# An attention and long-convolution kernel: the transform of 768 split into 3 by 256, with even and odd frequencies in separate rows

## The chip, the core and the metric

The kernel runs on one core of one Trainium2 chip. The metric is device microseconds for one launch. Five engines share the work: PE (matrix products), DVE (VectorE), ACT (ScalarE), POOL (GpSimd), and SP, which here only issues DMAs. Each engine works through its own instructions in order and waits on semaphores for the others.

## The reference, cut to what matters

```python
# q, k, v: [4, 8, 768, 64]; heads 0, 2, 6 see all earlier rows, the others 4 sink rows and a window of 64
a = softmax(mask(q @ k.T / 8)); x = (a @ v) as [4, 768, 512]
proj = x @ w_proj                      # [4, 768, 1536]
x1, x2, x3 = proj[..., :512], proj[..., 512:1024], proj[..., 1024:]
X2 = rfft(x2, n=768, axis=1)
H  = rfft(filter_fft, n=768, axis=0)
y  = x1 * irfft(X2 * H, n=768, axis=1) * x3
return y @ w_out                       # [4, 768, 512]
```

## The kernel before, in words

The work is 16 head pairs, numbered n, four to a batch b. A pair has two heads of one of three kinds: both see everything (RR), both are local (LL), or one of each (RL); the order in a batch is RR, LL, RL, LL. Everything is built in the function `patterned` as named operations; `run` issues them in the order of two lists of words, AHEAD and FAST. A word such as `E0.1/v` is operation E of pair 0, part 1, on VectorE (`/s` ScalarE, `/p` GpSimd), and `sc0.1@4` puts its result into PSUM banks from number 4. Each engine's queue is the list's order, kept to that engine's words; these lists were planned ahead, so the order of the whole kernel is fixed by hand, and a changed operation means a new list.

For a pair: `lq`, `lk`, `lv` load, `cq`, `ck`, `cv` cast to bf16, `T` and `E` turn q and k (from pair 8 on, T is a DMA transpose on SP's queue), `kx`, `ks`, `vx`, `vs` gather the keys and values that local heads need, `sc` makes scores, `ex` their exponentials on ScalarE (line 1471), `at` the products with the values (1516), `rec` and `nm` normalize (1522, 1533). Masks come in two ways: for pairs below BIASED_FAST, `sb` adds -32768 to scores by a product on PE (1465), and for the others `mk` and `mr` multiply the exponentials by 0 or 1 on VectorE or GpSimd (1484 to 1503).

Then comes the transform along the 768 rows, in a real form: `fd` and `fe` take the difference and the sum of the two halves of the rows, `fA`, `fS`, `fb`, `fr` combine thirds of these (1549 to 1561), and `W` multiplies by tables of cosines and sines on PE (1569 to 1573), `We` evicts. For each batch, `X` multiplies the spectrum by the middle third of w_proj (1620), in three parts t of two tiles of 512 channels, and `Xe` evicts to bf16. `pa`, `pb`, `pc` multiply by the spectrum of the filter (tile HAB) as complex numbers; in part 2, rows 0 to 63 hold one member of the pair and rows 64 to 127 the other, so that two DMAs `sw` swap halves of rows (1645) for `pb`. The inverse transform `c` is six products of 384 columns for each of four blocks of channels cb (1685), three for the even and three for the odd half; `ce` evicts one half to f32, `cv{b}.{cb}.0` and `.1` add and subtract (1696).

The projections x1 and x3 use `tn`, the attention result turned (by PE and `te`, or by a DMA transpose), four products of 384 columns for each half (1655); `xs` evicts x1 and `g` multiplies by x3 straight out of PSUM (1674). `y` multiplies by the convolution. `o` multiplies by w_out (1712), `oe` evicts and `st` stores (1732, 1734).

At the start the kernel makes its tables from sines (`fcol`, `turns`, `angle`, `wrap`, `size`, `sin`, `cos`, `G..`, `Gm..`, `Gh..`, `Gk..`, and `Gt`, `Ge`, which transpose the forward table for the inverse, 1227 and 1231), and transforms the filter: `lfilt`, `fold`, eighteen products `F` of 512 columns (1265), scalings `H` into HAB (1272, 1274), and two DMAs `Hd`. `blank` are products of nothing, laid among the first loads. The helpers `ev`, `two` and `scale` record their instructions at lines 971 to 978 and 1159 to 1163.

## Time and profile before

| | us |
|---|---|
| three timed runs | 195.18, 189.86, 193.86 (median 193.86) |
| the profiled execution | 190.27 |
| its span, first to last instruction | 188.4 |
| PE, DVE, ACT, POOL busy within the span | 176.5, 161.2, 145.6, 69.0 |
| mean granted TensorE clock | 0.985 |

The profile is one execution. Busy time is the union of an engine's instructions; ends of matrix products are modelled, so the pace of PE is better read from the chain of work that ended last, where products follow each other without a wait. In the groups of instructions a row gives line, engine, operation, output and input tiles, shapes and count, and behind the bar busy us, mean ns of one, and the idle time just ahead of them.

### The profile page before, as it was taken

The numbers are of one execution on the slowest core, as the hardware profiler recorded it, in microseconds if no ns is written. First come the engines' busy times: TensorE is split into PE (matmuls) and PEld (weight loads), VectorE is DVE, ScalarE is ACT, GpSimd is POOL, SyncE is SP. The second block draws the span as 40 slices with busy tenths as digits, with TensorE's granted clock in tenths as the row PEclk, the third lists the DMA queues.
The fourth block names the chain that finished last, engine by engine and source line by source line (L and its number), as shares of the span: only waits on it lengthen the run. The fifth ranks groups of instructions, "written<-read, shape, count | busy, mean of one in ns | idle before, by whom it ended". The sixth has DMA issues, their size and how long they took to land.

```text
span 188.4 us, 4493 instructions
## 1 busy us (share of the span) xinstructions
PE 176.5 (94%) x1694; PEld 103.4 (55%) x1694; DVE 161.2 (86%) x329; ACT 145.6 (77%) x210; POOL 69.0 (37%) x103
## 2 busy tenths in 40 slices
PE   7879999989998999999999999999999999999970
PEld 2437664647745563575555656655657765555530
DVE  6887799789889999999989999999899996499810
ACT  5787899999999999988989999696977332426360
POOL 5874785554322224670250460700650630000000
PEclk9978999999999999999999999999999999999997
DMA  4999999999999999999999989982162002312074
GB/s 152 330 274 279 208 197 236 270 286 251 213 202 225 215 185 166 233 219 213 202 233 228 228 221 238 250 87 56 60 98 111 3 2 111 135 36 111 11 286 157
DMA packets 78955, 34.01 MB, mean 180 GB/s; under 512 B 68306, under 2 KB 75218, under 8 KB 78930
## 3 DMA queue, kind: packets, MB, share of 16 engines
q1 hardware_dynamic: 75986, 30.81, 73.9%
q0 software_dynamic: 2944, 2.88, 9.1%
q8 instruction: 14, 0.23, 0.5%
q14 instruction: 11, 0.09, 0.2%
HBM read 24.64 MB, written 6.29 MB: 164 GB/s over the span
## 4 chain that ended last, share of the span: by engine, by line
PE 66%; ACT 14%; DVE 6%; DMA 5%; issue 3%; POOL 2%; SPq 2%; DVEq 0%; ACTq 0%; POOLq 0%
PE space L1655 18%; PE space L1712 11%; PE space L1620 8%; PE space L1452 7%; PE space L1685 7%; PE space L1516 6%; ACT f_pT L1471 4%; DMA f_qkT<-f_qk_bf 3%; ACT f_HAB L1274 3%; DMA f_v_f<-in_v_dram 2%; PE space L1465 2%; ACT f_qk_bf L975 2%; SPq L1383 2%; PE space L1569 1%; PE space L1571 1%
## 5 line engine op out<-in xcount | busy, mean ns | idle before, releaser
L1471 ACT ACTIVATE f_pT<-space 128x1024 bf16<-128x1024 f32 (+3 forms) x68 | 58.8, 917 | 6.1 <-PE space L1465 1.9
L1655 PE MATMUL space<-f_xT,f_wproj 128*128 128x384 bf16 x256 | 47.9, 326 | 0.1
L1655 PEld LDWEIGHTS <-f_wproj 128*128 128x128 bf16 x256 | 24.0, 98 | 17.1 <-issue 1.0
L1712 PE MATMUL space<-f_wout,r_gy 128*128 128x512 bf16 x96 | 24.7, 379 | 0.0
L1452 PE MATMUL space<-f_qkT 64*128 64x128 bf16 (+3 forms) x248 | 22.6, 253 | 1.1 <-DVE f_attn L1533 0.5
L1620 PE MATMUL space<-f_wproj,f_xh 128*128 128x512 bf16 x96 | 22.7, 379 | 0.1
L1685 PE MATMUL space<-f_Gi,r_P 128*128 128x384 bf16 x96 | 19.0, 326 | 0.7 <-ACT f_evs L975 0.3
L978 DVE TENSOR_TENSOR f_pT<-f_pT,r_mtab 128x1024 bf16<-128x1024 bf16 (+3 forms) x33 | 18.5, 583 | 0.8 <-ACT f_pT L1471 0.6
L975 ACT COPY f_o<-space 128x1024 f32<-128x1024 f32 (+1 forms) x12 | 9.9, 836 | 11.3 <-PE space L1712 11.2
L1516 PEld LDWEIGHTS <-f_pT 128*128 128x128 bf16 x472 | 16.7, 97 | 3.6 <-issue 0.9
L1516 PE MATMUL space<-f_v_aug,f_pT 128*128 128x65 bf16 x392 | 17.9, 193 | 0.6 <-ACT f_X L975 0.5
L1452 PEld LDWEIGHTS <-f_qkT 64*128 64x128 bf16 x248 | 10.3, 94 | 13.1 <-issue 10.4
L978 POOL TENSOR_TENSOR f_uv<-f_fo 128x256 bf16<-128x256 bf16 x12 | 9.1, 766 | 21.1 <-DVE f_fo L978 15.8
L1696 DVE TENSOR_TENSOR f_conv<-f_evs,space 128x384 bf16<-128x384 f32 x32 | 16.1, 545 | 0.6 <-PE space L1685 0.3
L975 ACT CAST f_xh<-space 128x768 bf16<-128x768 f32 x14 | 11.2, 808 | 4.9 <-PE space L1573 4.6
L1620 PEld LDWEIGHTS <-f_xh 128*128 128x128 bf16 x96 | 9.0, 98 | 10.0 <-issue 0.4
L1712 PEld LDWEIGHTS <-r_gy 128*128 128x128 bf16 x96 | 9.0, 98 | 8.9 <-issue 0.4
L1533 DVE TENSOR_TENSOR f_attn<-space,f_rec 128x768 bf16<-128x768 f32 x14 | 13.4, 955 | 0.4
L1685 PEld LDWEIGHTS <-r_P 128*128 128x128 bf16 x96 | 8.8, 97 | 7.4 <-issue 1.1
L978 POOL TENSOR_TENSOR f_fo<-f_attn 128x384 bf16<-128x384 bf16 x11 | 10.4, 960 | 2.4 <-DVE f_attn L1533 1.9
L975 ACT CAST f_X<-space 128x1024 bf16<-128x1024 f32 x8 | 8.2, 1020 | 2.8 <-PE space L1620 2.7
L978 POOL TENSOR_TENSOR f_pT<-f_pT,r_mtab 128x512 bf16<-128x512 bf16 (+1 forms) x6 | 6.8, 1146 | 9.1 <-ACT f_pT L1471 9.1
(136 smaller groups left out, 345.7 us busy)
## 6 DMA issues: line engine op xcount, KB each, us to landing
f_v_f<-in_v_dram SPq DMA_DIRECT2D x32, 192.0 KB, 4.7
out_dram<-f_o SPq DMA_DIRECT2D x9, 512.0 KB, 3.1
r_qk_f<-in_k_dram SPq DMA_DIRECT2D x10, 192.0 KB, 4.4
r_qk_f<-in_q_dram SPq DMA_DIRECT2D x10, 192.0 KB, 5.0
r_qk_f<-in_k_dram SPq DMA_DIRECT2D x4, 384.0 KB, 11.3
r_qk_f<-in_q_dram SPq DMA_DIRECT2D x4, 384.0 KB, 6.1
f_qk_f<-in_q_dram SPq DMA_DIRECT2D x4, 384.0 KB, 5.8
f_qk_f<-in_k_dram SPq DMA_DIRECT2D x4, 384.0 KB, 6.6
```

Source lines behind the costliest of these rows:

```text
L975: nc.scalar.copy(out=out, in_=in_)
L978: (nc.gpsimd if now["engine"] == "p" else nc.vector).tensor_tensor(out, a, b, op)
L1274: nc.scalar.activation(out=out_(), in_=in_(), func=AF.Copy, scale=w / S)
L1452: nc.tensor.matmul(sc[:, bank, col:col + 128 * cnt], lhsT=keys, rhs=qkT(n)[rows, 0, 128 * i:128 * (i + cnt)], start=(col == 0 or not biase ...
L1471: nc.scalar.activation(out=pT(n)[:, c, :, 0:w], in_=held[f"sc.{n}.{c}"][:, :, 0:w], func=AF.Exp, scale=SCALE)
L1516: nc.tensor.matmul(att[:, hh, 65 * i:65 * i + 65], lhsT=pT(n)[:, c, bank, col:col + 128], rhs=values, start=(z == 0), stop=(z == len(here) ...
L1533: nc.vector.tensor_mul(attn(n).rearrange("p i hh d -> p hh i d"), rows[:, :, :, 0:64], held[f"rec.{n}"][:, :, :, None].to_broadcast([128, ...
L1620: nc.tensor.matmul(ps[:, u, :], lhsT=xh(b)[:, cc, chain, 128 * part:128 * part + 128], rhs=wproj()[:, cc, DM:2 * DM], start=(cc == 0), sto ...
L1655: nc.tensor.matmul(ps[:, s, 0:HS], lhsT=wproj()[:, cc, part * DM + cb * 128:part * DM + (cb + 1) * 128], rhs=xT(b)[:, cc, s * HS:s * HS + HS],
L1685: nc.tensor.matmul(ps[:, 0, 0:HS], lhsT=P(b)[:, t, u, ch], rhs=Gi()[:, tile_no], start=(m == 0), stop=(m == 2))
L1696: fn(conv[:, half * HS:half * HS + HS], held[f"evs.{b}.{cb}"], held[f"c_ps.{b}.{cb}.1"][:, 0, 0:HS])
L1712: nc.tensor.matmul(ps, lhsT=gy(b)[:, cb, i * 128:(i + 1) * 128], rhs=wout()[:, cb, :], start=(cb == 0), stop=(cb == NC - 1))
```

## The change

The 768 rows are treated as 3 by 256. Frequencies of one parity are gathered in one set of rows, so that each of the three spectrum parts is a whole complex number per row: part 0 holds one class modulo 3, parts 1 and 2 the other two.

- Tables: a forward table of 6 tiles instead of 18, and two small inverse tables Gi and Gj of 256 columns, made straight from the sines. The steps skew, Gm, Gh and the transposes Gt with Ge are gone; the angle table is 512 columns wide instead of 384.
- Filter: it goes through the same sixths as the pairs (`fAF`, `fSF`, `fbF`, `frF`), 24 products `K` with evictions `Ke`, 24 transposes `F`, and scalings `H` of 512 columns. The DMAs `Hd` are gone. `gate` makes GpSimd wait for pair 3's q before the filter and weight loads.
- Pairs: `We` sorts the spectrum into six groups of 128. The forward products stay as they are.
- After the filter multiplication nine operations q form the three points of the transform of length 3: sums and differences of parts 1 and 2 (`qa`, `qs`), a correction of one row (`qr`), half of part 0 (`qh`), the sums (`qz`, `qb`, `qp`, `qm`) and a scaling (`qd`). The DMAs `sw` are gone.
- Inverse: for each cb six products of 256 columns instead of six of 384. In batches 0 to 2 `y` multiplies straight out of PSUM; in batch 3 ScalarE evicts first (`cv3.cb/s`). `ce` and the two halves `cv` are gone.
- The rows of the convolution now come sorted by class modulo 3: `xs` and `g` read x1 and x3 from PSUM with a step of three, and each store writes every third row of the output.
- BIASED_FAST 4 becomes 8: pairs 4 to 7 get their masks from PE (15 more `sb`) and lose `mk`, `mr`. Pair 14's `tn` becomes a DMA transpose.
- Both order lists are new, with other engines for some casts and evictions: among them three more `xs`, one more `nm`, one more `te` on ScalarE; on GpSimd four `mk` fewer, and `qa0`, `qd1`, `qd2`, `fbF` more. The blanks are still twelve in FAST, and now all stand among the first operations.

The core of the diff (the order lists cut to the end stage):

```diff
-TURNED_BACK = (0, 1, 2, 3, 4, 5, 6, 7, 14, 15)
+TURNED_BACK = (0, 1, 2, 3, 4, 5, 6, 7, 15)
-BIASED_FAST = 4
+BIASED_FAST = 8
+DIRECT = ((0, 0), (0, 1), (0, 2), (0, 3), (1, 0), (1, 1), (1, 2), (1, 3), (2, 0), (2, 1), (2, 2), (2, 3))
...
-X3.2.0 X3.1.0@0 Xe3.2/s X3.1.1 sw3.0 pa3.2/v sw3.1 x33.1.1 Xe3.1/s X3.0.0@2 g3.1 X3.0.1 pb3.1/v pa3.1/v
-x33.2.1@4 Xe3.0/s pb3.2/v o2.1.0@0 pa3.0/v o2.1.1 x13.3.1@6 pc3.1/v o2.0.0 pc3.2/v o2.0.1 x33.2.0 pb3.0/v
-oe2.1/s c3.0.0@2 pc3.0/v x13.3.0 st2.1 ce3.0/s g3.2 c3.0.1@3 xs3.3/s c3.1.1@0 cv3.0.0 c3.1.0@1 cv3.0.1 c3.2.0@2
...
+o2.4.0 o2.4.1 oe2.1/s X3.2.0@6 st2.1 X3.2.1 X3.1.0@0 Xe3.2/s X3.1.1 pb3.2/v X3.0.0@2 pa3.2/v Xe3.1/s x13.0.0@6
+pc3.2/v oe2.5/s pb3.1/v X3.0.1 pa3.1/v st2.5 x13.0.1 Xe3.0/s pc3.1/v x13.3.0@0 xs3.0/s pa3.0/v x13.2.0@4 qa3/v
+x13.3.1 pb3.0/v x33.0.0@2 xs3.3/s qs3/v x13.1.0@6 pc3.0/v qr3/s x33.0.1 qh3/v x13.1.1 g3.0 x33.1.1@0 qd3/s qb3/v
+x33.1.0 qz3/v x13.2.1 xs3.1/s qp3/v x33.2.1@2 xs3.2/s qm3/v x33.2.0 g3.1 c3.0@6 g3.2 c3.1@4 cv3.0/s c3.2@0
+cv3.1/s y3.0/v c3.3@2 cv3.2/s y3.1/v x33.3.1@6 cv3.3/s y3.2/v x33.3.0 y3.3/v o3.5.0@4 g3.3 o3.2.0@5 o3.5.1
...
+    def spectrum(ps, u, uv, br, ch):
+        nc.tensor.matmul(ps[:, u, 0:256], lhsT=br[:, 1, u, ch], rhs=G()[:, 3 * u:3 * u + 2], start=True, stop=False)
+        nc.tensor.matmul(ps[:, u, 0:256], lhsT=uv[:, 2 * u, ch], rhs=Gk()[:, u], start=False, stop=True)
+        nc.tensor.matmul(ps[:, u, 256:384], lhsT=br[:, 0, u, ch], rhs=G()[:, 3 * u + 2], start=True, stop=True)
+
+    def sorted_(x, ps):
+        ev(x.rearrange("p g (u j) -> p u g j", u=2), ps[:, :, 0:HS].rearrange("p u (g j) -> p u g j", g=6))
...
+            ps = banks(f"F_ps{t}", BF16, 1)
+            for c, g in enumerate(SPECTRUM[t]):
+                for cc in range(NC):
+                    nc.tensor.transpose(ps[:, 0, DM * c + 128 * cc:][:, 0:128], Hx()[:, cc, g], identity())
...
-                two(P(b)[:, t], held[f"X.{b}.{t}"], HAB()[:, t, 0:2], ALU.mult)
+                h = HAB()[:, t, 0:1].to_broadcast([128, 2, DM]) if t else HAB()[:, t, 0:2]
+                two(P(b)[:, t], held[f"X.{b}.{t}"], h, ALU.mult)
...
-                nc.sync.dma_start(out=Xw[to], in_=held[f"X.{b}.2"][at])
+        @op(f"qa{b}")
+            two(SD(b)[:, 0:2], P(b)[:, 1], P(b)[:, 2], ALU.add)
+        @op(f"qs{b}")
+            two(SD(b)[:, 2:4], P(b)[:, 1], P(b)[:, 2], ALU.subtract)
+        @op(f"qr{b}")
+            scale(SD(b)[0:1], flat(b)[0:1, 2:6], 2.0)
+        @op(f"qh{b}")
+            scale(Y0(b), P(b)[:, 0], 0.5)
+        @op(f"qz{b}")
+            two(Y0(b), Y0(b), SD(b)[:, 0:4:3], ALU.add)
+        @op(f"qd{b}")
+            scale(SD(b)[:, 1:3], SD(b)[:, 1:3], 2.0 * KAPPA)
+        @op(f"qb{b}")
+            two(P(b)[:, 0], P(b)[:, 0], SD(b)[:, 0:4:3], ALU.subtract)
+        @op(f"qp{b}")
+            two(flat(b)[:, 2:4], P(b)[:, 0], SD(b)[:, 1:3], ALU.add)
+        @op(f"qm{b}")
+            two(flat(b)[:, 4:6], P(b)[:, 0], SD(b)[:, 1:3], ALU.subtract)
...
-                    ps = banks(f"c_ps.{b}.{cb}.{r}", count=1)
-                    for m, (t, u, tile_no) in enumerate(INVERSE[r]):
-                        nc.tensor.matmul(ps[:, 0, 0:HS], lhsT=P(b)[:, t, u, ch], rhs=Gi()[:, tile_no],
-                                         start=(m == 0), stop=(m == 2))
+                for s, (re, im) in enumerate(POINTS):
+                    for c, rows in enumerate((re, im)):
+                        rhs = Gi()[:, c].rearrange("p a f -> p (a f)")[:, START[s]:START[s] + 256] if s else Gj()[:, c]
+                        nc.tensor.matmul(ps[:, 256 * s:256 * s + 256], lhsT=rows(b)[:, ch], rhs=rhs,
+                                         start=(c == 0), stop=(c == 1))
...
+                    nc.vector.tensor_mul(to, held[f"c_ps.{b}.{cb}"].rearrange("p a f -> p (a f)")[:, 0:S], x)
...
+                    rows = out[b].rearrange("(n p s) c -> s p n c", p=128, s=3)[i // 2]
```

469 lines of the change are left out of this document (227 added, 242 removed).

## The prediction

> **What bounds the kernel now.** I read the page's busy shares first, then the same by stage, cut where the bounding engine changes, then the chain for the true pace of PE.
>
> ```profile
> PE 176.5 (94%) x1694; PEld 103.4 (55%) x1694; DVE 161.2 (86%) x329; ACT 145.6 (77%) x210; POOL 69.0 (37%) x103
> ```
>
> ```profile
> 0.00:20.00 20.00, 17.10 (x130) 8.79 (x131) 15.43 (x40) 14.76 (x22) 13.82 (x37) 0.91 0.95 260
> 20.00:79.00 59.00, 55.65 (x664) 34.40 (x663) 53.61 (x108) 57.73 (x77) 26.27 (x34) 1.00 1.12 221
> 79.00:159.20 80.20, 80.20 (x780) 48.26 (x779) 74.92 (x156) 62.55 (x98) 28.89 (x33) 1.00 0.78 153
> 159.20:182.80 23.60, 23.53 (x124) 11.90 (x122) 17.20 (x27) 10.05 (x15) 0.00 (x0) 1.00 0.30 104
> 182.80:188.40 5.60, 0.00 (x0) 0.00 (x0) 0.00 (x0) 0.55 (x1) 0.00 (x0) 0.79 0.49 182
> ```
>
> The columns after the length are busy PE, weight loads, DVE, ACT, POOL. The reader is to see three regimes. From 20 to 79 us ScalarE works 57.73 of 59.00 us: its exponentials, casts and evictions set the pace. From 79 to 159.2 PE is full and DVE has 74.92 of 80.20. After 159.2 PE alone is full. At 182.8 PE is done; the last output tile and its store take 5.6.
>
> A full PE row can still hide slack, because matmul ends are modelled. The chain shows the pace when nothing waits:
>
> ```profile
> 20.18 1.30 PE space L1516 x42
> 28.13 0.34 PE space L1589 x6
> 30.45 1.51 ACT f_HAB L1274 x2
> ...
> 75.41 0.94 DVE f_conv L1696 x2
> ...
> 83.19 4.58 PE space L1655 x28
> ...
> 144.00 0.49 PE space L1685 x3
> 159.16 0.86 PE space L1620 x4
> 177.55 5.19 PE space L1712 x24
> ```
>
> The columns are start and length. A product of 65 columns takes 31 ns, 128 columns 56, 384 columns 163, 512 columns 216; 256 columns, which stand on that line, I take at 108. The ACT and DVE rows show that consecutive instructions overlap: two conv halves take 0.94 us, not twice 0.545. I subtract 0.085 us from each duration below when I add a queue. Counted with these paces along the order list, PE's whole work is 158.0 us, of which 58.2 stand ahead of the last exponential of head pair 8 and 99.8 behind it.
>
> ```profile
> 78.33 0.60 ACT L1471 ACTIVATE f_pT<-space 128x512 bf16<-128x512 f32 x1
> ```
>
> This row of the timeline is that exponential, done at 78.9 us. PE finishes 103.9 us later: only 4.1 us of slack for 99.8 of work. The 21 us that PE loses lie before it, under ScalarE's regime.
>
> **The change part by part.** The prices come from these groups (busy us, mean ns):
>
> ```profile
> L1696 DVE TENSOR_TENSOR f_conv<-f_evs,space 128x384 bf16<-128x384 f32 x32 | 16.1, 545 | 0.6 <-PE space L1685 0.3
> L975 ACT CAST f_xh<-space 128x768 bf16<-128x768 f32 x14 | 11.2, 808 | 4.9 <-PE space L1573 4.6
> L978 DVE TENSOR_TENSOR r_P<-r_P,f_m 128x1024 bf16<-128x1024 bf16 x12 | 8.2, 687 | 0.1
> L971 DVE COPY f_qkT<-space 128x768 bf16<-128x768 bf16 x8 | 7.6, 950 | 0.9 <-PE space L1407 0.9
> L1674 DVE TENSOR_TENSOR r_gy<-r_x1s,space 128x768 bf16<-128x768 bf16 x8 | 7.5, 942 | 0.3 <-PE space L1655 0.3
> L978 DVE TENSOR_TENSOR f_uv<-f_fo 128x256 bf16<-128x256 bf16 x20 | 7.5, 392 | 0.1
> L975 ACT COPY f_evs<-space 128x384 f32<-128x384 f32 x14 | 6.8, 493 | 3.1 <-DVE f_conv L1696 2.2 <-PE space L1685 0.8
> L975 ACT CAST f_qk_bf<-r_qk_f 128x768 bf16<-128x768 f32 x8 | 6.5, 831 | 1.0 <-DMA r_qk_f<-in_q_dram 1.0
> L975 ACT COPY f_qkT<-space 128x768 bf16<-128x768 bf16 x8 | 6.2, 802 | 0.1
> L978 DVE TENSOR_TENSOR r_gy<-f_conv,r_gy 128x768 bf16<-128x768 bf16 x10 | 5.7, 569 | 0.1
> L1530 ACT ACTIVATE f_attn<-space,f_rec 128x64 bf16<-128x64 f32 x24 | 5.1, 344 | 0.0
> L971 DVE COPY f_xT<-space 128x768 bf16<-128x768 bf16 x8 | 4.3, 550 | 0.6 <-PE space L1589 0.6
> L1274 ACT ACTIVATE f_HAB<-space 128x1024 bf16<-128x1024 f32 x2 | 2.1, 1041 | 0.1
> L1274 ACT ACTIVATE f_HAB<-space 128x512 bf16<-128x512 f32 x2 | 1.2, 598 | 0.0
> L975 ACT COPY f_Gi<-space 128x768 bf16<-128x768 bf16 x1 | 0.8, 793 | 0.0
> ```
>
> PE, whole program. The 96 inverse products shrink from 384 to 256 columns: 96 x 0.055 = -5.3 us. The 18 table transposes go (-1.0) and pair 14's six go to a DMA transpose (-0.3). The filter's 18 products of 512 (3.9) become 16 of 256, 8 of 128 and 24 transposes (3.5). The bias products of pairs 4 to 7 are new: 12 of 128 columns, twice 2816 columns, 2176 columns, +3.9. Sum about -3.0; by the list, 155.1 us. The blanks stay twelve plus the first one: nothing.
>
> Front, up to the exponentials of pair 8. Both order lists hold the same exponentials there, so what counts is the rest of ScalarE's queue. Gone: four filter scalings of 1024 and one of 512 (4.1 + 0.6), the table's eviction (0.8) and three table steps (1.3, estimated from their 256 and 384 elements), three f_evs copies (1.5), eight casts (6.6), six evictions of 768 (4.8), two small copies (0.6): 20.3 us in 28 instructions, 17.9 without overlaps. New: five evictions of 768 (4.0), three casts (2.5), three filter evictions Ke (2.4), pair 0's normalization as twelve small activations (half of 5.1), one more scaling of 1024 (qd0, 1.0), four of 512 less the halving of one (2.4 - 0.4), table steps (2.1), two small copies (0.6): 17.2, or 15.3 without the overlaps of 22. Net -2.6 us of a queue that is 98% busy, so the front ends that much earlier. ScalarE's waits ahead of the first exponentials (14.76 busy in the first 20 us) could move by 1.5 either way; I take 0, since more table work fills them but also has to come first. Front: -2.6, between -4.0 and -0.5. The filter's longer way (fold, sixths, K, Ke, transposes, scalings) lies under these exponentials; pair 4 to 7's masks leave DVE at no cost to ScalarE.
>
> Middle, to the last batch's spectrum (79 to 159.2 us before). On PE, 99.8 us behind pair 8 become 97.1, of which the end stage gives 0.3: -2.4. On DVE, 19 conv halves go (19 x 0.46 = -8.8); eight y at 0.48 become twelve reading PSUM, which I price as the row that multiplies a PSUM tile, 0.86 (+6.4); 14 sums and differences of 1024 (qa to qm) at 0.60 and a one-row scaling come (+9.2); casts, x1 evictions and transposed copies that the new list gives to ScalarE and POOL leave (about -5.5). Net +1.4 on 74.92 busy. ScalarE gets the load: 82 operations for 76 in 80 us at 62.55 busy, room enough. So the stage lies between PE's answer, 80.2 - 2.4 = 77.8, and DVE's if it keeps its 5.3 us of idle time and adds 0.5 for waits on POOL (below): 82.1. DVE is the engine whose work grows, so I lean to it by two thirds: 80.7, +0.5.
>
> End stage. PE still has six spectrum products (5.2 us), seven pairs of x1/x3 products (9.1), then inverse, the rest of x3, and output: 23.3 for 23.6. What is new is the chain: spectrum of part 2 ready after 1.7, evicted at 2.8; DVE then does ten sums of 0.60 with a wait of 0.5 for the third eviction, 9.3; qr on ScalarE, one row of 2048, 1.9 by the slope from 512 to 1024 (0.44 per 512), 11.2; DVE's qb, qz, qp, qm 2.4: the inverse can start 13.7 us after the stage's start. PE has products until 14.3. So it is hidden with 0.6 in hand; if the cover is short the loss is one for one. -0.3, between -0.3 and +2.0. The swap DMAs go:
>
> ```profile
> f_Xw<-r_X SPq DMA_DIRECT2D x8, 128.0 KB, 3.1
> ```
>
> and with them the wait of their reader:
>
> ```profile
> L978 DVE TENSOR_TENSOR f_m<-f_Xw,f_HAB 128x1024 bf16<-128x1024 bf16 x4 | 2.7, 682 | 0.0
> ```
>
> DVE was never idle ahead of that reader, so the swap was hidden and I give its removal nothing; SP's queue loses eight issues that waited for an eviction, and gains tn14, late, when the DMA engines stand at a share of 0.3 to 0.8. Stores now write every third row, still 2 KB each: nothing, up to +0.5. Reading PSUM with a step of three: f_qkT's copy above, which steps through PSUM and writes with a step, takes 950 against f_xT's 550 straight, so on bf16 a step costs 0.4; but g and x1 read f32, already 942, and ScalarE takes 0.80 with the step (f_qkT) as without (f_xh). Nothing.
>
> Sum: -2.6 + 0.5 - 0.3 = -2.4 on the profiled execution, 190.27 us (span 188.4 and 1.9 around it): 187.9. Of the three runs shown one lies at 189.86, two at 193.86 and 195.18; the median is 1.9% above the profiled one, so the range's upper part also covers that scatter.
>
> **Rivals.** First, PE keeps the middle and DVE fills its idle time: front -2.6, middle -2.4, end -0.3, 185.0. For it: the stage row shows PE unbroken from 79 us on. Against: DVE's 93%.
>
> Second, the two-input operations collide with POOL:
>
> ```profile
> 82.67 1.83 POOL L978 TENSOR_TENSOR f_fo<-f_attn 128x384 bf16<-128x384 bf16 x2
> 82.85 0.87 DVE L978 TENSOR_TENSOR f_uv<-f_fo 128x256 bf16<-128x256 bf16 x1
> ```
>
> That f_uv took 0.87 against a mean of 0.39, and ended when POOL's first sum had (two took 1.83). In the middle such DVE operations fill 36.1 us and grow by the 8.4 us of q sums less 3.9 of y: 41.3 by the list, with some sums moved over from POOL, beside 27.1 us of POOL. Exclusive, the two need 68.4 of some 78 us in fixed orders: DVE keeps idle and waits, the middle gains nothing and loses 1.9 to 3: front -2.6, middle +2.4, end -0.3, 189.8. For it: the rows. Against: in the middle DVE still finds 5.3 us in which it waits for others.
>
> The Trainium skill, "SBUF — State Buffer", section "SBUF: two separate sides", says that VectorE, in a two-port mode or with two SBUF inputs, and GpSimd exclude each other for a whole instruction. By that rule this rival is the rule here, and the rows above agree with it.
>
> Third, on the other side: slices and broadcasts cost the new sums their fast rate. Place: pa of parts 1 and 2 (filter broadcast) and qz, qb (every third slot of SD). Price: by f_qkT against f_xT 0.40 per 768 elements, 0.53 per 1024, four a batch. The middle gets ten of them, +5.3, on DVE's +1.4 and 0.5: 82.1 of work in a stage of 80.2 and some 2 of idle, +3.9; the end's chain gets 2.1 less 0.6 in hand, +1.5; -2.6 + 3.9 + 1.5 = +2.8, 193.1. It decides from 0.33 us per sum, where 14 of them cost what front, idle time and cover give (2.6 + 1.4 + 0.6). Against it stand the masks, which broadcast as pa will:
>
> ```profile
> L978 DVE TENSOR_TENSOR f_pT<-f_pT,r_mtab 128x1024 bf16<-128x1024 bf16 x12 | 8.1, 697 | 0.0
> ```
>
> They run at 0.70, the plain r_P sums at 0.69: long inner runs, which f_qkT's lack.
>
> **How the numbers follow.** Forecast 187.9, chance 0.42; PE's answer 185.0, 0.25; collisions 189.8, 0.20; slow rate 193.1, 0.13. The bounds of the parts give 183.6 (-4.0, -2.4, -0.3) to 193.7 (-0.5, +1.9, +2.0); leaving one in ten out at each side, 184.0 to 193.2; the forecast's own range is 186.2 to 189.6. About 2% (3.8 us, that is below 186.5 or above 194.1) is what a measurement of this kernel can tell from no change. Faster by over 2%: PE's answer and a fifth of the forecast, 0.33. Slower: half of the slow rate and part of the collisions with a late chain, 0.12. Within: 0.55.
>
> **What would show it.** Front: pair 8's last exponential at 76.3 instead of 78.9, ScalarE still 98% busy before it; later than 78 and the front is wrong. Middle: DVE busy 76 to 77 us between there and the last spectrum; under 75 with PE unbroken means the first rival. r_P sums near 1.1 us instead of 0.69 mean the third; many at 0.69 and some at 1.5 beside POOL mean the second. The y rows that read PSUM at 0.94 or my 0.86 is wrong. End: L1712's 24 products unbroken, inverse products starting about 14 us after X3.2. A gap of PE before the last inverse, a first exponential after 14 us, or a wait of X0's sums for the filter would break the forecast.

## The result, and the profile after

The changed kernel is slower: 193.76 us median of four runs (191.98 to 195.70) against 191.88 for the kernel before beside it, ratio 1.0122 (95% interval 1.0081 to 1.0163). In two of its four runs TensorE's granted clock stood at 0.970 and the time above 195; the ratio and the profile are from the others (clock 0.983, 192.0). The profiled execution took 192.03 us, span 190.2, against 190.27 and 188.4. The forecast was 187.9. The interval is clear of 1, but the loss is smaller than the 2% that the prediction names as what a measurement can tell.

The page's busy times of the changed kernel, to be set beside the first row of the prediction:

```profile
PE 175.6 (92%) x1733; PEld 106.5 (56%) x1733; DVE 154.7 (81%) x309; ACT 153.1 (80%) x226; POOL 75.1 (39%) x111
```

VectorE has 6.5 us less to do than before, TensorE 0.9 less (2.9 by the list), and the span is longer: somewhere engines wait. By stage, with the cuts of the prediction (columns: length, then busy PE, weight loads, DVE, ACT, POOL, granted clock):

```profile
0.00:20.00 20.00, 17.19 (x136) 8.28 (x137) 12.84 (x38) 17.56 (x27) 13.73 (x39) 1.00 0.97 272
20.00:79.00 59.00, 54.08 (x663) 35.73 (x660) 48.01 (x92) 50.63 (x76) 32.90 (x43) 0.97 1.13 221
79.00:159.20 80.20, 78.96 (x794) 48.41 (x793) 76.69 (x154) 67.34 (x105) 28.43 (x30) 1.00 0.67 140
159.20:182.80 23.60, 23.44 (x141) 13.40 (x140) 16.48 (x25) 16.38 (x19) 0.00 (x0) 1.00 0.18 71
```

In the second row ScalarE works 50.63 us where it worked 57.73. It has idle time now, and the stage did not get shorter. The two events that cut the stages, from the timeline (last exponential of head pair 8) and the chain (spectrum of the last batch):

```profile
79.74 1.06 ACT L1494 ACTIVATE f_pT<-space 128x1024 bf16<-128x1024 f32 x1
```

```profile
160.96 4.32 PE space L1629 x20
```

They stand at 80.80 us (its end) and 160.96 us, so the front ends at 80.8 (before 78.9, forecast 76.3): +1.9 instead of -2.6. The middle takes 80.2 us (before 80.3), the end 29.2 from the last spectrum (before 29.2). The whole loss is in the front. How busy was ScalarE up to that exponential? The first row is the kernel before, the second the one after:

```profile
0.00:78.90 78.90, 72.64 (x792) 43.16 (x793) 68.94 (x147) 72.41 (x97) 40.09 (x70) 0.98 1.08 231
```

```profile
0.00:80.80 80.80, 73.04 (x821) 45.23 (x822) 62.64 (x133) 69.99 (x105) 46.63 (x81) 0.98 1.10 234
```

ScalarE's work fell by 2.4 us, as counted (-2.6). Its idle time grew from 6.5 to 10.8, +4.3, although it had less of it in the first 20 us. The sum is +1.9. The question is what it waits for. Between 20 and 80.8 us, where it idles 8.4 us, the table of waits puts 7.8 of them down to TensorE; from 20 us to the same exponential the kernel before had 1.2. What TensorE waits for is in the chain of the changed kernel between 20 and 48 us:

```profile
20.59 0.12 POOL f_gate L1234
20.71 12.07 DMA r_gy<-in_moe_filter_fft_dram
32.81 1.83 DVE r_gy L976 x2
34.63 0.20 DVE f_v_x L969
34.83 0.60 DVE r_P L976
35.43 0.47 DVE f_qk_bf L969
35.90 0.61 DVE r_P L976
36.57 1.11 issue
37.68 0.24 DVE f_rec L1545
37.94 0.97 DVE f_attn L1556
38.95 0.27 PE space L1280
...
46.52 0.89 PE space L1306 x16
47.41 0.65 PE space L1694 x4
```

The filter lands at 32.8; VectorE folds it and makes its sums, and only then the quotient of pair 2 (37.94), for which TensorE waits. The prediction had put this under the exponentials. In the kernel before, the filter's load was issued at 14.9 and that quotient started at 35.34.

From 38.95 on the chain stays on TensorE. The filter's products (L1280 to L1282) and transposes (L1306) stand there directly ahead of the first projection products (L1694, x1), which the timeline has from 47.25 us; in the kernel before, the filter's products ran from 29.6 to 37.1 us and the projections began at 42.04. From 40 to 70 us TensorE of the changed kernel is busy 30.00 of 30 us (before 28.58). So what comes late ahead of 39 us is not made up behind it: VectorE's order, the loads and TensorE's own queue are all suspects.

TensorE also pauses before that, and its clock falls:

```profile
30.00:35.00 5.00, 2.96 (x47) 2.48 (x48) 2.49 (x5) 5.00 (x7) 0.00 (x0) 0.85 1.17 251
35.00:40.00 5.00, 3.39 (x46) 2.81 (x43) 4.69 (x7) 3.74 (x7) 3.42 (x2) 0.81 1.22 198
40.00:45.00 5.00, 5.00 (x64) 3.96 (x65) 4.60 (x8) 4.34 (x6) 4.56 (x7) 1.00 1.22 195
```

Clocks of 0.85 and 0.81 over 5 us each are 3.4 us at half speed in all (0.15 x 5 x 2 and 0.19 x 5 x 2). The Trainium skill, "TensorE: Matmul & The Clock Gate", section "What's actually happening", gives the half clock after an idle window of about 3.4 us. The length agrees: the stretch at half clock is 33.45 to 36.87 us. But TensorE's longest pauses here, by the table of waits, were 1.9 and 1.4 us, and in the 3.4 us ahead of that stretch it was busy 1.40, so a window with pauses in it was enough.

### The profile page after: what moved, and what is told of

It is laid out like the page before. It is cut to its first block, busy times and chain, and to the rows that moved or that the text cites. A ratio compares the mean times of both kernels' runs of the same rounds, so it can differ in the third digit from the quotient of the medians.

```text
span 190.2 us, 4548 instructions
## 1 busy us (share of the span) xinstructions
PE 175.6 (92%) x1733; PEld 106.5 (56%) x1733; DVE 154.7 (81%) x309; ACT 153.1 (80%) x226; POOL 75.1 (39%) x111
## 4 chain that ended last, share of the span: by engine, by line
PE 45%; DVE 31%; ACT 9%; DMA 6%; issue 5%; POOL 2%; DVEq 0%; POOLq 0%
PE space L1694 13%; PE space L1629 8%; PE space L1747 7%; DMA r_gy<-in_moe_filter_fft_dram 6%; DVE r_P L976 6%; PE space L1475 4%; DVE f_pT L976 4%; DVE f_attn L1556 3%; PE space L1488 3%; PE space L1539 3%; DVE r_gy L1736 2%; DVE r_gy L1713 2%; PE space L1280 2%; ACT f_conv L973 2%; PE space L1281 1%
## 5 line engine op out<-in xcount | busy, mean ns | idle before, releaser
L1694 PE MATMUL space<-f_xT,f_wproj 128*128 128x384 bf16 x256 | 46.2, 326 | 0.2
L1694 PEld LDWEIGHTS <-f_wproj 128*128 128x128 bf16 x256 | 24.1, 98 | 16.4 <-issue 1.2
L1475 PEld LDWEIGHTS <-f_qkT 64*128 64x128 bf16 x248 | 10.6, 94 | 18.0 <-issue 14.9
L1539 PEld LDWEIGHTS <-f_pT 128*128 128x128 bf16 x472 | 17.9, 100 | 3.2 <-issue 1.0
L1539 PE MATMUL space<-f_v_aug,f_pT 128*128 128x65 bf16 x392 | 19.1, 198 | 0.1
L973 ACT COPY f_o<-space 128x1024 f32<-128x1024 f32 (+1 forms) x13 | 11.5, 888 | 8.4 <-PE space L1747 8.4
L971 POOL COPY f_v_x<-f_v_aug 64x520 bf16<-64x520 bf16 (+1 forms) x11 | 6.0, 553 | 20.4 <-DVE f_v_aug L969 10.1
L976 DVE TENSOR_TENSOR f_pT<-f_pT,r_mtab 128x512 bf16<-128x512 bf16 (+3 forms) x23 | 13.3, 588 | 0.1
L1488 PE MATMUL space<-f_btab,r_identity 128*128 128x128 bf16 (+2 forms) x66 | 12.8, 287 | 0.0
L976 POOL TENSOR_TENSOR f_uv<-f_fo 128x256 bf16<-128x256 bf16 x10 | 6.9, 698 | 13.9 <-DVE f_fo L976 9.5
L969 DVE COPY f_qkT<-space 128x768 bf16<-128x768 bf16 x8 | 7.5, 950 | 4.0 <-PE space L1475 2.0
L1280 PE MATMUL space<-r_G,f_br 128*128 128x256 bf16 x32 | 9.0, 281 | 1.4 <-DVE f_attn L1556 1.4
## 6 DMA issues: line engine op xcount, KB each, us to landing
f_v_f<-in_v_dram SPq DMA_DIRECT2D x32, 192.0 KB, 4.9
r_qk_f<-in_k_dram SPq DMA_DIRECT2D x10, 192.0 KB, 4.4
r_qk_f<-in_q_dram SPq DMA_DIRECT2D x10, 192.0 KB, 4.1
```

The source lines that it names most:

```text
L969: nc.vector.tensor_copy(out=out, in_=in_)
L973: nc.scalar.copy(out=out, in_=in_)
L976: (nc.gpsimd if now["engine"] == "p" else nc.vector).tensor_tensor(out, a, b, op)
L1280: nc.tensor.matmul(ps[:, u, 0:256], lhsT=br[:, 1, u, ch], rhs=G()[:, 3 * u:3 * u + 2], start=True, stop=False)
L1475: nc.tensor.matmul(sc[:, bank, col:col + 128 * cnt], lhsT=keys, rhs=qkT(n)[rows, 0, 128 * i:128 * (i + cnt)], start=(col == 0 or not biase ...
L1488: nc.tensor.matmul(held[f"sc.{n}.{c}"][:, bank, 128 * at:128 * (at + width)], lhsT=identity(), rhs=btab()[:, what:what + width], start=Fal ...
```

## The experiments

All kernels here are edits of the changed kernel but one (e9). The edits are to the order list, where a word is an operation. Ratio is to the kernel before on the same chip, with its 95% interval; the other columns are from each profiled execution, in us: time at half clock between 25 and 65 (e1, e2 and e5 have 5.2, 6.8 and 2.2 more outside that window), end of the quotient of pair 4, span, and the span less that end.

| run | ratio | half clock | pair 4 | span | rest |
|---|---|---|---|---|---|
| before | 1 | 0 | 53.9 | 188.4 | 134.5 |
| after | 1.0122 [1.0081, 1.0163] | 3.4 | 55.2 | 190.2 | 135.0 |
| e1_filter_early | 1.0445 [1.0361, 1.0529] | 1.6 | 62.9 | 197.4 | 134.5 |
| e2_masks_back | 1.0466 [1.0382, 1.0551] | 10.2 | 60.0 | 199.3 | 139.3 |
| e3_warm | 1.0108 [1.0068, 1.0149] | 0 | 57.4 | 191.7 | 134.3 |
| e4_no_filter | 1.0100 [1.0050, 1.0149] | 3.4 | 54.7 | 189.1 | 134.4 |
| e5_weights_first | 1.0520 [1.0454, 1.0586] | 8.0 | 61.4 | 200.0 | 138.6 |
| e6_nofilter_weights_first | 0.9986 [0.9953, 1.0019] | 3.4 | 54.6 | 189.3 | 134.7 |
| e7_no_bias | 1.0078 [1.0039, 1.0117] | 6.8 | 57.9 | 191.3 | 133.4 |
| e8_wout_late | 1.0237 [1.0180, 1.0295] | 6.8 | 57.8 | 192.2 | 134.4 |
| e9_before_wout_late | 0.9972 [0.9929, 1.0015] | 0 | 53.5 | 188.6 | 135.1 |
| e12_quotients_ahead | 1.0267 [1.0198, 1.0335] | 6.8 | 60.7 | 195.0 | 134.3 |
| e13_nm4_ahead | 1.0299 [1.0243, 1.0354] | 0 | 55.7 | 191.1 | 135.4 |
| e14_ahead_wout_late | 1.0189 [1.0122, 1.0257] | 6.8 | 58.3 | 192.9 | 134.6 |
| e15_no_filter_late_fill | 1.0142 [1.0092, 1.0192] | 3.4 | 55.5 | 191.6 | 136.1 |
| e16_loads_out | none | 3.4 | 56.9 | 192.9 | 136.0 |
| e18_both_limits_out | 1.0077 [1.0030, 1.0124] | 0 | 52.2 | 189.8 | 137.6 |

The last column is the main reading. In eleven of the seventeen rows it lies between 134.3 and 135.4, the kernel before included: there, what moves the quotient of pair 4 moves the end by about as much. It is no rule: e7 has 133.4, the other five between 136.0 and 139.3, and e10, e11 and e17, which are not in the table, between 145.5 and 149.0. Behind that quotient the two kernels differ by 0.5 (134.5 and 135.0); 1.3 of the 1.8 us arise ahead of it.

Another mark is as good or better where it holds: the start of the first projection products. The span less that start is 142.9 to 143.2 us in eight kernels (after, e1, e3, e4, e8, e12, e13, e14), although the start itself lies anywhere from 45.9 to 54.3. The other edits in the table have 142.0 (e7) or 144.7 and more. The kernel before has 146.4 from 42.04 on, the changed one 143.0 from 47.25 on: 5.2 us later up to there, 3.4 shorter behind it.

Each profile is one execution, and the load of the filter landed at 32.8 us in the changed kernel, at 33.7 in e7 and at 34.2 in e3, although their lists leave it where it was. Differences below about 1 us between two single profiles can be such scatter, and the split into 1.3 and 0.5 is no surer than that.

### Four single suspects

The filter's load (gate and load) put earlier into GpSimd's queue:

```
-cq4/p E1.0/v ... at0.1@6 gate E4.0/s lfilt at0.0
+cq4/p gate lfilt E1.0/v ... at0.1@6 E4.0/s at0.0
```

> The changed kernel with the filter load (gate, lfilt) moved up in GpSimd's queue, behind the cast of pair 4's q, so that it is issued near 15 us instead of 20.7 and lands near 27 instead of 32.8. Late-filter theory (VectorE stands behind fold1 until the load lands, pair 2's normalization and PE's W0.1 come late, and PE runs at a lower clock after its pause): the wait of 1.8 us ahead of fold1 goes, PE's pause of 1.7 us ahead of W0.1 shrinks, the time falls by 2 to 4 us to 188 to 190, level with the kernel before. Front-products theory (PE has more to do in the front: masks of pairs 4 to 7 and the filter's products): the pause goes but the time falls by less than 1 us, since PE is full from 40 us on.

It took 198.81 us. The move did not test what it was meant to: the load was issued at 19.8 instead of 20.7 and landed at 31.6 instead of 32.8. The gate waits for a load of q, and GpSimd's casts stood behind it, as GpSimd's timeline shows:

```profile
19.65 0.18 POOL L1231 COPY f_gate<-f_qk_f 1x1 f32<-1x1 f32 x1 [5.54 <-DMA f_qk_f<-in_q_dram]
```

Of the 7.7 us lost at the quotient of pair 4, 7.2 come out at the end.

The masks of pairs 4 to 7 on VectorE and GpSimd again, as before the change:

```
-BIASED_FAST = 8
+BIASED_FAST = 4
-sb4.0 ... sb7.2
+mk4.0/v mk4.1/v mk4.2/p mk5.0/v ... mk7.2/v mr6/v
```

> The changed kernel with BIASED_FAST 4: the 15 added mask products of pairs 4 to 7 (3.9 us of PE) go, and twelve mask products by VectorE and three groups on GpSimd come back behind the exponentials. Late-filter theory: no gain, or under 1 us; the pause at 30 to 39 us stands. Front-products theory: PE ends the front 3 to 4 us earlier and the time falls by 2.5 to 3.5 us to 188.5 to 189.5; if VectorE becomes the bound instead (it gets 5 us more), it rises by up to 2.

199.49 us. With fewer products TensorE ran 10.2 us at half clock within the table's window, and the filter landed 1.1 us later. The run does not support the bias products as the loss, but with so much half clock, and the masks on VectorE again, it does not clear them either.

Fourteen blank products in TensorE's two pauses:

```
-T6.0@7 ... W0.1@2
+blank13@7 T6.0@7 ... blank14@1 W0.1@2
```

> The changed kernel with 14 blank products in PE's two pauses: eight ahead of T6.0 (near 30 us) and six ahead of W0.1 (near 37 us). Late-filter theory with the clock as its larger part: the granted clock between 30 and 40 us rises from 0.81 to 0.85 to 1.0, the 22 products of 65 columns there run at 31 ns again, and the time falls by 1.5 to 2.5 us. If the clock is not what costs (front-products theory or the waits themselves): no change, or 0 to 1 us slower by the blanks.

192.46 us: the half clock went (1.00 throughout), the time did not. But in this run the filter happened to land 1.4 us later, and VectorE's timeline shows the quotient of pair 2 later by the same 1.4:

```profile
34.17 1.83 DVE L974 TENSOR_TENSOR r_gy<-r_gy 128x1536 bf16<-128x1536 bf16 x2 [3.11 <-DMA r_gy<-in_moe_filter_fft_dram]
...
39.30 0.96 DVE L1554 TENSOR_TENSOR f_attn<-space,f_rec 128x768 bf16<-128x768 f32 x1
```

From fold to quotient 5.1 us, as after the change (32.81 to 37.94). What the half clock alone costs, this run does not show.

The filter's transform left out:

```
-fold1/v ... fold0/v ... fAF/v ... K0.0 ... F0 ... H2.5/s
+hset0 hset1 hset2
+            nc.gpsimd.memset(HAB()[:, t], 0.01)
```

> The changed kernel without the filter's transform: folds, sixths, K, Ke, F and H are left out, and GpSimd fills HAB with a constant (the filter is still loaded). It shows all that the filter's longer way costs. Late-filter theory: VectorE's 6 us at 31 to 38, the pauses and the slow clock go, pairs 2 to 5 move up by 4 to 6 us, and the time falls by 4 to 6 us to 186 to 188. Front-products theory: 3.5 us of PE work go with it, so 3 to 4 us. If neither (the loss lies in the middle): under 1.5 us.

192.36 us, hardly less, though the quotient of pair 2 ended at 36.2 instead of 38.9. So the filter's chain is not the only limit: TensorE now waited 2.3 us for the projection weights, and VectorE for v of pairs 4 and 6.

### Loads and the bias products

```
-gate ... lfilt ... lw0.0 ... lwo ... lw2.0 lw2.1 lw1.0 lw0.1 lw1.1
+gate lw0.0 lw0.1 lw2.0 lw2.1 lw1.0 lw1.1 lfilt lwo
```

e5 has this order and the filter's work further back; e6 this order on top of e4; e7 is the changed kernel without `sb4.0` to `sb7.2` and without masks in their place.

> The changed kernel with the projection weights (six loads, 1.5 MB) issued ahead of the filter's load, the output weights last, the filter's two folds, sixths, products and transposes put behind the attention of pairs 2 and 3 and behind the first projection products; nothing left out. Theory 'TensorE idle between 30 and 42 us' (in the changed kernel it was 6.35 us busy of 10 there, because the quotients of pairs 2 and 3 stood behind the filter's folds on VectorE and the weights landed only at 44.9, and from 40 us on TensorE is busy without a gap until 75 us): quotient of pair 2 ends near 36.5 instead of 38.9, of pair 3 near 39.8 instead of 41.3, quotient of pair 4 near 53 instead of 55.2, end of the span 2 us earlier, 190 us. Rival 'the front is a chain of exponentials on ScalarE and the order of the filter does not count': within 0.5 us of the changed kernel, 192. Rival 'the filter's late landing is needed': later than the changed kernel, 194, because VectorE waits for HAB before the first products.

> As the run without the filter's transform (the table of filter rows filled with a constant), with the projection weights issued ahead of the filter's load. Leaves out the filter's transform, so the output is not the reference's. Without the filter alone the time fell by only 1 us, because TensorE then waited at 45.9 us for the weights. Theory 'weights late, then TensorE is the bound': TensorE's 3.5 us of filter products are now saved in full and the first projection products start near 42 us: 187 to 188 us. Rival 'something else, the exponentials or a load of q and k, holds the front': again 191 to 192 us.

> The changed kernel without the bias products of pairs 4 to 7 and without any mask in their place; leaves out the masking of those pairs, so the output is not the reference's. The prediction costed these 3.9 us of TensorE at nothing, as lying beside exponentials. Theory 'TensorE is the bound from 40 to 77 us': 3 to 4 us less, 188 to 189 us. Rival 'the prediction's price': within 0.7 us of the changed kernel, 192.

e5 took 201.73 us. In its order the gated rows of batch 0 are written over the filter's spectrum, with which they share a buffer, so its filter is not the reference's; and the filter's evictions stood ahead of the exponentials of pair 5. It brought the quotient of pair 2 to 36.6 as expected and decides nothing else.

e6 took 190.28, level with the kernel before and by the medians 2 us below e4. Its first projection products started at 44.6 instead of 45.9, where e4 had waited 2.3 us for weights. The two profiled executions, however, have the same quotient of pair 4 and the same span, so where the 2 us lie they do not show. What then stood ahead of that quotient is in VectorE's timeline:

```profile
47.08 0.56 DVE L965 CAST f_v_aug<-f_v_f 128x768 bf16<-128x768 f32 x1 [1.54 <-DMA f_v_f<-in_v_dram]
48.78 0.56 DVE L965 CAST f_v_aug<-f_v_f 128x768 bf16<-128x768 f32 x1 [1.14 <-DMA f_v_f<-in_v_dram]
...
51.28 0.95 DVE L965 CAST f_xh<-space 128x768 bf16<-128x768 f32 x1
52.69 0.76 DVE L965 CAST f_qk_bf<-r_qk_f 128x768 bf16<-128x768 f32 x1
53.62 0.96 DVE L1557 TENSOR_TENSOR f_attn<-space,f_rec 128x768 bf16<-128x768 f32 x1
```

The casts of v of pairs 4 and 6 wait for their loads; behind the second stand an eviction of x1, the gate, the spectrum's eviction (51.28), a cast and the quotient of pair 4 (last row).

e7 took 193.01: without 3.9 us of bias products it is 0.4% below the changed kernel, and the two intervals overlap. Its filter landed 0.9 us later, it ran 3.4 us longer at half clock, and the last column shows 1.6 us regained behind pair 4. So there they do cost something; what they cost in all at an even clock no run shows.

### The output weights' load, and VectorE's order

e8 and e9 move `lwo` (512 KB) to near 54 and 49 us, in the kernel after and in the one before. e10 moves `cv6/v kx7/v ck9/v` behind `nm4/v`, and e11 does both.

> The changed kernel with the load of the output weights (512 KB, used by the output products alone) issued behind the last cast of v of pair 5, near 54 us, instead of at 22 us between the loads of the projection weights; nothing left out. Theory 'loads': in both kernels the loads of v of pairs 4 to 6 stand in the DMA queues behind the filter and the weights and land at 45 to 50 us, and their casts hold VectorE and the quotient of pair 4, so 512 KB less ahead of them (about 2 us at the 260 GB/s of that stretch) bring v of pairs 4 and 6 to 43.5 to 46.5 us, the quotient of pair 4 from 55.2 to about 53.5 us and the time down by 1 to 2 us, 190 to 191. Rival 'TensorE's order is the bound from 40 us on': the loads land earlier and the time stays at 192.

> The kernel before with the same move of the output weights' load, behind the cast of v of pair 4 near 49 us. Theory 'loads': its cast of v of pair 6 on VectorE waited for the landing at 46.2 us and that of pair 4 on GpSimd for 47.9, so it gains 1 to 2 us too, ratio 0.99 to 0.995; then the loads are a limit of both kernels, and the difference between them lies in what stands on VectorE between the landing and the quotient. Rival 'the kernel before is bound by the exponentials on ScalarE, which was busy 4.9 of every 5 us': no change, ratio 1.0.

> The changed kernel with the cast of v of pair 6, the sums over k of pair 7 and the cast of k of pair 9 put behind the quotient of pair 4 on VectorE; nothing left out. Theory 'VectorE's order behind the loads': in the changed kernel the quotient of pair 4 began 0.8 us after its sums were done because these stood ahead of it, one of them waiting for its load; quotient of pair 4 1 to 1.5 us earlier, time 1 us less. Rival 'TensorE's order': within 0.5 us of the changed kernel.

> The changed kernel with both moves. Theory 'loads, then VectorE's order': the gains add, 189.5 to 190.5 us, level with the kernel before. Rival 'TensorE's order': 191.5 to 192.

e8 was slower, 194.60 us. The loads of v came earlier (pair 6 at 46.0 instead of 48.6), but a second stretch at half clock, 39 to 43 us, came with a filter that landed 0.55 later:

```profile
30.00:35.00 5.00, 3.09 (x43) 2.48 (x44) 1.93 (x3) 5.00 (x7) 0.00 (x0) 0.75 1.17 255
35.00:40.00 5.00, 2.58 (x34) 2.11 (x32) 4.93 (x9) 3.43 (x6) 2.86 (x1) 0.84 1.22 198
40.00:45.00 5.00, 5.00 (x54) 4.18 (x53) 3.25 (x7) 3.01 (x4) 3.50 (x6) 0.72 1.18 213
```

e9 changed nothing (190.34): in the kernel before v of pair 6 landed 1.6 us earlier and its cast started at 47.04 instead of 47.39. So this load did not hold the kernel before.

e10 and e11 took 204.21 and 204.25 us and decide nothing: the load of pair 12, which goes into the buffer of pair 9, stood ahead of the moved cast, so pair 9 got pair 12's keys and the cast waited 11.87 us for them.

### The filter's sums behind the quotients

```
-fold1/v fold0/v vs3/v fAF/v cq5/v fSF/v frF rec2 nm2/v fbF/p ... nm3/v
+fold1/v fold0/v vs3/v cq5/v rec2 nm2/v fAF/v fSF/v ... nm3/v frF fbF/v
-K1.0@2 ... tn3@1
+tn3@1 K1.0@2
```

e12 is this; e13 also puts `kx7/v ck9/v lk12` behind `nm4/v`; e14 adds the late `lwo`; e15 is e4 with the constant fill near 52 us.

> The changed kernel with the filter's sixths behind the quotient of pair 2 and its last two sums (the second now on VectorE instead of GpSimd) behind that of pair 3, and the transposes of pair 3 ahead of the filter's products; nothing left out. Theory 'filter in front of the quotients': in four runs the quotient of pair 2 ended 6.4 to 6.5 us after the filter landed (32.5 to 38.9, 33.0 to 39.5, 33.8 to 40.3, 33.4 to 39.8), whatever else was changed, and TensorE's next products wait for it; with only the two folds left ahead of it, it ends near 36.5, pair 3 near 39.7, the loss of 1.4 us in TensorE at 39 us goes, and the time falls by 1.5 to 2 us, 190 to 190.5. Rival 'loads of v hold the front at 50 us': those two quotients are earlier, that of pair 4 stays at 55, and the time stays at 192.

> The run before this one of the same call (the filter's sums behind the quotients) and, besides, the sums over k of pair 7 and the cast of k of pair 9 behind the quotient of pair 4 on VectorE, with the load of pair 12 into the same buffer behind that cast. Theory 'VectorE's order behind the loads': 0.5 to 0.9 us less than that run. Rival: no change against it.

> The filter's sums behind the quotients, as in the first run of this call, and the output weights' load issued near 54 us. In the run with that late load alone the loads of v landed 1 us earlier, as expected, and the time still grew by 2 us, with a second stretch of half clock at 39 to 42 us. Theory 'half clock after TensorE's idle time': without the wait for the filter's sums there is no second stretch, and the time is 0.5 to 1 us below the first run of this call, 189.5. Rival 'the late load itself costs, later on': 1 us or more above the first run.

> The changed kernel without the filter's transform, the filter table filled with a constant by GpSimd behind the sums over v of pair 5 near 52 us; leaves out the filter's transform, so the output is not the reference's. In the earlier run without the transform the fill stood at 31 to 36 us, and two small sums of VectorE took 1.9 and 2.0 us beside it instead of 0.25. Theory 'filter in front of the quotients': quotient of pair 2 near 36.3, of pair 3 near 38.8, time 189 to 190.5. Rival 'loads': as the earlier run, 192.

195.96, 195.82, 193.96 and 193.17 us: the gain did not come in any. e13's profiled execution (192.97 us, the fastest of its seven, and without half clock) shows why for itself: the quotients of pairs 2 and 3 ended at 36.0 and 39.9, 2.9 and 1.4 us earlier, but TensorE now waits for the filter's last sums, 0.62 us at 41.1 and 0.92 at 42.4. So the first projection products started at 48.2 instead of 47.3, and the quotient of pair 4 stayed at 55.7. Why the other six executions took 2 to 4 us more the profile does not show. e12 and e14 lost more to half clock (42 to 49, and 32 to 36 with 43 to 46). The expectation that those two quotients alone set the front is refuted. e15, at 55.5, had its fill beside a copy and a cast of VectorE.

### Both limits out

e16 combines e15, the weights first, the late `lwo` and eight blank products at 30.5 us; e17 is a full kernel with the same loads and the filter's work behind pair 5; e18 is e16 with the fill on VectorE:

```
-            nc.gpsimd.memset(HAB()[:, t], 0.01)
+            nc.vector.memset(HAB()[:, t], 0.01)
```

> The changed kernel without the filter's transform (table filled with a constant at 52 us; the output is not the reference's), the projection weights issued ahead of the filter, the output weights' load near 54 us, and eight blank products of 512 columns in TensorE's idle time at 30.5 us to keep its clock. Theory 'two limits side by side': in the changed kernel the quotient of pair 4 (55.2 us, and the end of the span follows it by 134.3 to 135.4 us in nine runs) is held both by the filter's chain over VectorE and TensorE and by the landing of v of pair 6 (48.3) and k of pair 9 (51.0), whose casts stand ahead of it on VectorE; taking out one left it at 54.6 to 55.7. With both out of the way it ends near 52.5 and the span near 187, time 188.5. Rival 'TensorE's order alone': 54.5 again, time 191.

> The changed kernel in full with the same order of the loads and the same blank products; the filter's folds behind the transposes of pair 3, its sixths behind the cast of v of pair 4 and the quotient of pair 4, its products and transposes behind the attention of pair 5, its sorted spectrum in the buffer of the products P instead of the gated rows'. Theory 'two limits side by side': quotient of pair 4 near 53, the filter table ready near 64 us, just as the first products need it, time 189 to 190, level with the kernel before or 0.5 us below. Rival 'the filter's 4 us of TensorE and its evictions cost the same wherever they stand': 191 to 192.

> As the run with the loads and the filter's chain both out of the way (no filter transform, so the output is not the reference's; projection weights first, output weights' load near 54 us, eight blank products at 30.5 us), with the constant fill of the filter table on VectorE in its idle time behind pair 4's and pair 5's sums instead of on GpSimd at 50 us, where one cast of VectorE (768 elements, float32 to bfloat16) took 5.76 us beside it. Theory 'two limits side by side': nothing is ahead of the quotient of pair 4 but the landing of v of pair 6 at 45 to 46 us; gate and evicted spectrum end at 50 us as there, the quotient of pair 4 at 51.5 to 52, the span 134.3 to 135.4 us after it, 186 to 187.3, time 187.7 to 189, ratio to before 0.985 to 0.993. Rival 'TensorE's order alone, whatever lands when': 54.5 and 191.

e16 ran between 191.06 and 195.51 us; its profile is of an execution of 194.72, so its expectation is not decided. VectorE's timeline and then GpSimd's:

```profile
50.03 5.76 DVE L965 CAST f_qk_bf<-r_qk_f 128x768 bf16<-128x768 f32 x1
55.71 0.21 DVE L1546 RECIPROCAL f_rec<-space 128x12 f32<-128x12 f32 x1
55.96 0.96 DVE L1557 TENSOR_TENSOR f_attn<-space,f_rec 128x768 bf16<-128x768 f32 x1
```

```profile
50.09 5.29 POOL L1235 MEMSET f_HAB<- 128x2048 bf16 x3
```

The cast, 0.6 us elsewhere, lasted as long as the fill.

e17 took 204.39 us (ratio 1.0770, 1.0699 to 1.0841). The buffer I gave the spectrum also holds the sums that it is made from, so its filter is other data. Its quotient of pair 4 came at 53.7, as expected; then the filter's evictions, on both engines ahead of the first products, put that of pair 6 at 88.6 instead of 76.0. At that place the filter's work is not free either.

e18 tells most about the front. Its VectorE timeline, to be set beside e6's, and the start of its first projection products:

```profile
44.85 1.97 DVE L965 CAST f_v_aug<-f_v_f 128x768 bf16<-128x768 f32 x2
48.12 0.95 DVE L1714 TENSOR_TENSOR r_gy<-r_x1s,space 128x768 bf16<-128x768 bf16 x1 [0.33 <-PE space L1695]
49.02 0.96 DVE L965 CAST f_xh<-space 128x768 bf16<-128x768 f32 x1
50.33 0.76 DVE L965 CAST f_qk_bf<-r_qk_f 128x768 bf16<-128x768 f32 x1
51.27 0.96 DVE L1557 TENSOR_TENSOR f_attn<-space,f_rec 128x768 bf16<-128x768 f32 x1
```

```profile
43.97 4.06 PE L1695 MATMUL space<-f_xT,f_wproj 128*128 128x384 bf16 x24 [0.50 <-ACT f_pT L1495]
```

The quotient of pair 4 ends at 52.2: 3.0 us before the changed kernel's, 1.7 before the old one's. With the filter alone out and v still late (e4, e6, e15) it had stayed at 54.6 to 55.5; with the loads alone earlier and the filter in (e8, e14) it was at 57.8 and 58.3, a second stretch at half clock included. e18 differs from e6 by three things, the late `lwo`, the blank products that keep the clock, and the place of the fill. Its projections start 0.6 us earlier than e6's (43.97 and 44.58), so the clock can be at most 0.6 of the 2.4 us between their quotients; the rest is the time for which VectorE of e6 waits for v (1.54 and 1.14). The time, however, was 191.83 us, ratio 1.0077, not 188, and above e6's 190.28: the lead shrank to 1.5 us by the quotient of pair 7, in a stretch where VectorE worked 27.91 of 30 us, 5.3 of them my fill, whose second and third parts stand in the chain. So the forecast of the quotient nearly held (51.5 to 52), and the forecast of the time did not; what the span would be without the fill was not measured.

## Why the prediction was wrong, point by point

**The step that failed** is the front's: "Net -2.6 us of a queue that is 98% busy, so the front ends that much earlier", with its companion "The filter's longer way ... lies under these exponentials". The net was right (-2.4). The inference was not: ScalarE idles 4.3 us more, and the front ends at 80.8, where the prediction says "later than 78 and the front is wrong". That ScalarE alone set the pace before had been read from its busy share. The chain of the kernel before leaves it for two loads that are no part of ScalarE's work, so other limits stood close even there:

```profile
62.15 4.20 DMA f_v_f<-in_v_dram
68.63 5.61 DMA f_qkT<-f_qk_bf
```

In the changed kernel 7.8 of ScalarE's 8.4 us of idle time behind 20 us are waits for TensorE. What comes too late for TensorE is the filter's chain: load issued at 20.7 instead of 14.9, folds and sums on VectorE 5.1 us ahead of the quotient of pair 2, then the filter's products and transposes on TensorE directly ahead of the first projections (47.25 instead of 42.04). The other loads come later too: the projection weights land by 47 us instead of 38, v of pair 6 at 48.6 instead of 46.5, with its cast ahead of the quotient of pair 4 on VectorE. Nothing waits for these loads yet, since VectorE is full from 46.7 to 55.2 and TensorE from 40 on; they are the next limit. Without the filter's chain they hold the quotient at 54.6 (e6, where the casts wait) instead of 55.2, and with both out it ends at 52.2 (e18). The +1.3 at that quotient and 0.5 behind it are the 1.8 us by which the span grew. How much of the 1.3 the 3.4 us at half clock are stays open, since e3, without them, had a later filter. So does the share of TensorE's own queue: e7 took products away, but lost clock. And no full kernel got both limits out of the way, so that the front ends late is shown, and that these two limits are all of the cause is argued.

I had looked at SP's and GpSimd's queues only for what the change added and removed, not for the place that the new list gave to the loads that were already there. "a wait of X0's sums for the filter would break the forecast" named the right input but the wrong reader.

**ScalarE's first waits.** The prediction let them "move by 1.5 either way" and took 0. ScalarE was busy 17.56 of those 20 us, and the quotient of pair 0 ended at 24.8 instead of 22.8, that of pair 1 at 24.9 instead of 27.2; between them the 0 that I took is as good as any.

**TensorE.** 155.1 us of work counted; busy 0.9 less on the page, the stretch at half clock included. What the bias products cost is not shown (e7).

**The middle** came out close in the sum, 80.2 us for a forecast 80.7, but not by the way that was forecast. Between the two events that the prediction names, 80.80 and 160.96 us, VectorE is busy 74.89 us (before 75.03), not "76 to 77"; the 76.69 of the stage row belongs to the cuts of the kernel before. So the growth that the forecast leaned on did not come, and TensorE, busy 78.95 of these 80.16 us, was not unbroken either: the sign of the first rival, under 75 with TensorE unbroken, is half met. Which engine set this stage no run tested, and the near hit is partly luck. The y rows that read PSUM took 0.95, not 0.86.

**The end** came out at 29.2 against 29.2 instead of 0.3 less; the first inverse product followed the last spectrum's start by 14.3 us ("about 14"). These rows of the chain show it, and the output products with one short pause:

```profile
166.79 8.45 PE space L1694 x52
175.24 0.67 PE space L1721 x6
...
180.62 4.07 PE space L1747 x18
```

**The rivals.** The slow rate is refuted: sums of slices and of the broadcast filter run at 0.69 in the groups of the changed kernel, like the plain ones.

```profile
L976 DVE TENSOR_TENSOR r_P<-r_P,f_SD 128x1024 bf16<-128x1024 bf16 x12 | 8.0, 683 | 0.0
L976 DVE TENSOR_TENSOR r_P<-f_X,f_HAB 128x1024 bf16<-128x1024 bf16 x8 | 5.5, 687 | 2.6 <-ACT f_X L973 2.5
```

"PE keeps the middle" did not happen: the middle stayed at 80.2. Whether collisions with GpSimd had a part in it was not tested. That the loads and the filter arrive later than the exponentials was not on the list of rivals.

## What to carry to other kernels

A queue at 98% is the bound only while its inputs come in time: before work taken off it is counted as a gain, the next-latest inputs (each load's landing, each sum ahead of the consumer on its engine) have to be timed too. When a change rewrites an order list, the loads that it leaves in number but moves in place belong in the sum. Two limits side by side hardly show in a run that removes one of them, and a stand-in that fills a buffer is work too and has to be put where its engine idles.

## What was not expected of the hardware

A cast of 768 elements on VectorE took 5.76 us beside three GpSimd fills of 1.8 us each (e16), against 0.61 as the mean of five in the changed kernel. The Trainium skill, "SBUF — State Buffer", section "SBUF: two separate sides", says that a VectorE operation in a two-port mode and a GpSimd one shut each other out for a whole instruction. That this cast is in such a mode no run shows by itself, but its length agrees with it; in e16 the cast did not get in between the three fills, while in e15, beside the same three, a cast took 2.08 us and ended with the first. On GpSimd itself a scaling of 1024 elements took 2.77 us, against 0.42 on VectorE and 1.05 on ScalarE:

```profile
L1186 POOL TENSOR_SCALAR f_SD<-f_SD 128x1024 bf16<-128x1024 bf16 x2 | 5.5, 2768 | 11.3 <-ACT f_SD L1188 8.5 <-DVE f_SD L1184 2.7
L1184 DVE TENSOR_SCALAR f_Y<-r_P 128x1024 bf16<-128x1024 bf16 x2 | 0.8, 425 | 0.0
L1188 ACT ACTIVATE f_Y<-r_P 128x1024 bf16<-128x1024 bf16 x2 | 2.1, 1047 | 0.0
```

And taking products away from TensorE went with more time at half clock: 6.8 us with 3.9 us of bias products less (e7), or 10.2 with masks in their place (e2), instead of 3.4. The filter also landed later in both, by 0.9 and 1.1 us, so which of the two brought it is not shown.
